# A gated mix of linear and softmax attention: output products and values stored from ScalarE's queue, head rows loaded in one transfer, 52 units of row maxima in the front instead of 56, and a new written order

## Chip, cores and metric

The kernel runs on 1 core of one Trainium2 chip. The metric is the device time of one execution in microseconds (us). Before the change it is 1009.66 us, the median of 3 runs (1009.21 to 1011.46).

## The reference

One sequence of S = 2048 tokens, D = 448 channels, H = 16 heads of 28. The output mixes two attentions of the same x by a gate for each token, all in fp32:

```
qkv = x @ wqkv                                   # for A and for B, each its own weights
A:  phi(u) = [softmax(u w_phi), softmax(-u w_phi)]          # 56 features for each head
    o = phi(q) (phi(k)^T v) / (phi(q) sum(phi(k)) + 1e-6);  a = o @ woA
B:  p = softmax(q k^T * 28^-0.5);  o = p v;                 b = o @ woB
g = sigmoid(sum(x * gate_w));  out = g * a + (1 - g) * b
```

## The kernel before

**Two parts.** The *front* (to about 333 us) computes everything of A, the projections of B, the gate, and a first share of B's row maxima. The *main loop* (s = 0 to 271, one *slot* each) computes B's attention: 4 groups of 4 heads x 4 blocks of 512 queries x 16 tiles of 128 keys are 256 slots. The products of the front are taken in split fp32r: each factor is written as a high and a low part, and high x high, high x low and low x high are summed (`x3`, L128, `tok_major`, L136).

**One slot of the main loop.** TensorE makes four score tiles `st` of 128 keys x 512 queries (`score_group`, L1010, matmul at L1048), ScalarE takes the exponential `p` (L1051), and TensorE adds the values, `pv` (`values`, L1136, matmuls at L1143). Key tiles are read from *stacks* `kst`: one stack holds four key tiles (512 keys) of one group; five stacks go round, and two query stacks `qst`. `stack` (L814) zero-fills one on POOL (L816), `load_k` (L835) and `load_q` (L825) load it from the scratch tensor `qk_d` in DRAM (L821, four transfers each), and the first one is copied from `qk0` (L838). Slots 0 to 3 use the first key stack, slots 4 to 7 the second (`kst1`), 8 to 11 the third, 12 to 15 the fourth. The values lie in `vb0` (key tiles 0 to 7) and `vb1` (8 to 15), loaded by `load_early` (L804, transfer at L808, 2048 KB each) from the scratch tensor `v_d`, into which `value_b` (L787) stored them tile by tile (`ve`, copied by ScalarE at L800, stored at L802).

**Row maxima.** The softmax of B subtracts the row maximum of q k^T, so the maxima of a block of queries are needed ahead of its scores. They are computed from q k^T a second time, in two forms that do the same work:

- in the front as *units* (`mx_unit`, L279): four matmuls at L305 into `pmb` and `pmd`, a relu by ScalarE (L312) of 128 x 1024, two fused add-and-max instructions of DVE (L314). NF = 56 units are in the front.
- in the main loop as *visits* (`mx_visit`, L329): four matmuls `pm` (L346), a relu by ScalarE (L350), two reductions and a fused one by DVE (L354, L357). The rest of the maxima are 200 visits: one in each slot below TWO = 167, beyond it one in each second slot.

The trick of both: max(a, b) = b + relu(a - b), with a - b from *differences of keys*. For a visit these are `kc` tiles: `mx_load` (L204) loads 28 rows of each of four heads (`mx_rows`, L191, transfers at L194), and POOL subtracts `kd` from one head's rows (L214, first to be used in visit s = 1, 2, 3 for `kc0_0`, `kc0_1`, `kc0_2`). Query rows are loaded likewise by `mx_query` (L221, `qc`).

**What sets the order.** The front's order is a list of strings, written by hand (from L940; each letter is a step, its number the tile): "o2.1" computes a tile of A's output (`out_a`, L628: the passes `poa`, then ScalarE multiplies by the gate into `ga`, L634, which is stored in `ga_d` at L635), "v15" a tile of values, "m", "c", "n", "r" parts of A's normalization (among them the products `oU` by `rsa`, L448, and the low parts `lo`, L592), "t" transposes (`turn`, L553), "z" loads the first stacks, "y" loads `vb0`, "l" opens the tiles for the last units. From "w" on, units are put between matmuls by a table `at` (L925): a unit goes in when as many passes (of 214) of outputs and values have been issued as its next number says. Engines other than SP run their instructions in this order. SP's order is made by the scheduler, and all transfers of this kernel, those of `ga`, `ve` and `vb` too, are issued by SP.

The order of the steps that open the main loop is also written out: four key stacks and a query stack are made (five fills), `load_k(0, 1)` and `load_early(1, 8)` follow, then the last two units and the scores of slot 0.

Of the kernel before, what the change touches and what calls it, by code (L numbers as in the profile page):

```python
# [29 lines left out]
NF = 56  # L30
# [10 lines left out]
def gated_mix_kernel(ctx, tc, xT, wqkB, wvB, wvA, wkAT, wqAT, phi, woA, woB,  # L41
# [34 lines left out]
    qk_d = dr.tile([2 * D, 2, S], F32, tag="qkd", name="qkd")  # L76
# [114 lines left out]
    def mx_rows(r, rows, src, heads, c):  # L191

        for i, j in zip(rows, heads):
            nc.sync.dma_start(f32(r[32 * i:32 * i + DH]), src[DH * j:DH * j + DH, 0, c:c + 512])  # L194
        return r
# [25 lines left out]
    def mx_query(gq):  # L221
        g, qb = divmod(gq, NQ)
        mxs[("qc", gq)] = mx_rows(mx_tile("qc", f"qc{gq}", 3), range(4), q_d[g], range(4), qb * 512)

    def pair_load(g, c):
# [5 lines left out]
        mx_rows(r, (0, 1), k_d[g], heads, b * 1024)  # L231
        mx_rows(r, (2, 3), k_d[g], heads, b * 1024 + 512)
        mx_rows(t, (2, 3), k_d[g], heads, b * 1024)
# [9 lines left out]
    def pair_query(gq, hp):  # L243
        g, qb = divmod(gq, NQ)
        mxs[("qp", gq, hp)] = mx_rows(mx_tile("qc", f"qp{gq}_{hp}", 3), range(4), q_d[g],
                                      (2 * hp, 2 * hp + 1) * 2, qb * 512)
# [381 lines left out]
    def out_a(n, a):  # L628
# [6 lines left out]
        nc.sync.dma_start(ga_d[n][a], ga)  # L635
# [56 lines left out]
    def first_units():  # L692
# [3 lines left out]
        for b in range(4):  # L696
            nc.sync.dma_start(raw[b][:, 0, :], wqkB[:, b, :512])
            nc.sync.dma_start(raw[b][:, 1, :], xT[:, b, :512])
# [4 lines left out]
        for _ in range(8):  # L703
# [30 lines left out]
    for n in range(4, NP):  # L734
# [9 lines left out]
        if n == 14:  # L744
            part_loads("wvA", wvA, 450, "wvA")
            nc.sync.dma_start(sel_s, sel)
            nc.vector.memset(gate1, -1.0)
# [39 lines left out]
    def value_b(t, mid=None):  # L787
# [13 lines left out]
        if t in EARLY:  # L801
            nc.sync.dma_start(v_d[:, k], v)  # L802

    def load_early(i, n):  # L804

        k = [t // 8 for t in EARLY].index(i)
        nc.gpsimd.memset(vb[i][:, 0, 0:1, 28:29], 1.0)
        nc.sync.dma_start(vb[i][:, :n].rearrange("p t h d -> p t (h d)"), v_d[:, k:k + n])  # L808
# [118 lines left out]
    do = {"p": query, "f": feature2, "t": turn, "v": value, "e": take_exps, "n": numer,  # L927
# [11 lines left out]
    for w in (  # L939
# [38 lines left out]
    TWO = 167  # L978
# [75 lines left out]
    kst += [stack(f"kst{i}", True) for i in range(1, 5)]  # L1054
    qst.append(stack("qst1", False))
# [4 lines left out]
    load_early(1, 8)  # L1060
# [313 lines left out]
```

## Time and profile before

| | |
|---|---|
| median of 3 runs | 1009.66 us (1009.21 to 1011.46) |
| the profiled execution | 1010.6 us, its span 1008.8 us, granted clock 0.998 |
| front, to the first scores `st` | 333.28 us of the span |
| main loop and end | 675.5 us of the span |
| busy: TensorE / ScalarE / VectorE / POOL | 990.9 / 794.6 / 674.2 / 233.4 us |

A row of a timeline gives the start, the length, the engine, line, operation, output and inputs of neighbouring instructions of one kind; the bracket is the idle time of the engine ahead of them and what ended it. A row of a table of stretches gives the window, its length, the busy time of PE, PEld (weight loads, beside PE), DVE, ACT and POOL with the number of instructions, the granted clock, the busy share of the DMA engines and GB/s. SPq is the time in which SP's queue issues transfers.

### The profile page before, as it was taken

The page shows a single profiled execution, that of the slowest core. Times are in us where ns is not written, and L with a number is a line of the kernel's source. Part 1 is how long each engine was busy: PE and PEld are TensorE (multiplying, and loading weights), DVE is VectorE, ACT ScalarE, POOL GpSimd, SP SyncE. Part 2 cuts the span into 40 slices and gives each one's busy share as a digit, 9 for nine tenths or more (in the row PEclk, how much of TensorE's full clock was granted, in tenths as well). Part 3 has the DMA queues.
Part 4 walks back from the last instruction along what each step waited for, and adds up shares of the span by engine and source line. Part 5 has one row for each costly group of instructions (what it writes and reads, how often), then busy time and mean ns, then how long its engine had stood idle before and what let it go on. Part 6 is the DMA issues. An engine that isn't in the chain of part 4 may idle for free.

```text
span 1008.8 us, 18258 instructions
## 1 busy us (share of the span) xinstructions
PE 990.9 (98%) x6604; PEld 549.4 (54%) x6604; DVE 674.2 (67%) x1351; ACT 794.6 (79%) x1491; POOL 233.4 (23%) x229
## 2 busy tenths in 40 slices
PE   9999999999998989999999999999999999999998
PEld 8877777898766433333333333333334444455656
DVE  6567767687857568888888788888886444544202
ACT  5456555544466889999999999999999999979672
POOL 1265445686811410210120101102011011101010
PEclk9999999999999999999999999999999999999999
DMA  8975220513358762332614323343233364315131
GB/s 301 317 248 176 97 88 31 191 62 101 107 153 241 211 144 49 79 77 60 129 59 109 78 51 90 85 110 90 62 86 76 82 127 107 89 37 148 62 104 55
DMA packets 73076, 115.18 MB, mean 114 GB/s; under 512 B 19641, under 2 KB 31593, under 8 KB 72713
## 3 DMA queue, kind: packets, MB, share of 16 engines
q1 hardware_dynamic: 72986, 114.02, 40.3%
q8 instruction: 52, 0.85, 0.4%
q14 instruction: 38, 0.31, 0.1%
HBM read 77.88 MB, written 35.68 MB: 113 GB/s over the span
## 4 chain that ended last, share of the span: by engine, by line
PE 89%; DVE 4%; DMA 3%; POOL 2%; issue 1%; ACT 1%; SPq 0%; DVEq 0%; POOLq 0%; ACTq 0%
PE st L1048 27%; PE pv L1143 24%; PE pm L346 8%; PE pqk L125 6%; PE pk L144 4%; PE pva L144 4%; PE pq L125 3%; PE pob L125 3%; PE pvb L144 2%; PE pmb L305 2%; PE poa L125 2%; PE pqk L722 1%; DMA kst<-qkd 1%; DMA vb<-vd 1%; PE pn L565 1%
## 5 line engine op out<-in xcount | busy, mean ns | idle before, releaser
L1051 ACT ACTIVATE p<-st 128x512 f32<-128x512 f32 x1020 | 527.7, 641 | 27.0 <-PE st L1048 26.8
L357 DVE TENSOR_REDUCE part<-pm 128x1 f32<-128x512 f32 x450 | 287.5, 685 | 157.4 <-PE pm L346 157.4
L1143 PE MATMUL pv<-p,vb 128*32 128x512 f32 x2048 | 264.5, 604 | 0.0
L350 ACT ACTIVATE rl<-pm 128x512 f32<-128x512 f32 x200 | 124.4, 622 | 18.8 <-PE pm L346 17.8
L346 PEld LDWEIGHTS pm<-kc,qc 28*128 28x128 f32 x800 | 38.8, 182 | 171.4 <-issue 100.6
L448 POOL TENSOR_TENSOR oUb<-oUb,rsb 128x512 f32<-128x512 f32 x15 | 19.3, 1289 | 457.1 <-DMA rsb<-rdb 138.6
L1048 PE MATMUL st<-qk,kst 128*128 128x512 f32 x384 | 116.9, 426 | 0.9 <-DVE part L357 0.9
L1048 PE MATMUL st<-qst,kst 128*128 128x512 f32 x384 | 114.9, 423 | 0.0
L346 PE MATMUL pm<-kc,qc 28*128 28x512 f32 x800 | 102.1, 496 | 2.8 <-POOL kc L214 2.8
L354 DVE CUSTOM_DVE_ANT_0 rl<-pm,rl 128x512 f32<-128x512 f32 x150 | 102.2, 681 | 0.0
L1143 PEld LDWEIGHTS pv<-p,vb 128*32 128x32 f32 x2048 | 47.4, 108 | 95.7 <-issue 88.9
L1048 PEld LDWEIGHTS st<-qk,kst 128*128 128x128 f32 x384 | 64.2, 188 | 39.4 <-ACT p L1051 16.8
L1048 PEld LDWEIGHTS st<-qst,kst 128*128 128x128 f32 x384 | 64.3, 187 | 38.1 <-ACT p L1051 16.6
L314 DVE CUSTOM_DVE_ANT_0 rl<-pmb,rl 128x512 f32<-128x512 f32 x72 | 46.0, 677 | 23.6 <-ACT rl L312 23.6
L125 PE MATMUL pqk<-XH,wB 128*128 128x512 f32 x192 | 59.6, 397 | 0.0
L312 ACT ACTIVATE rl<-pmd 128x1024 f32<-128x1024 f32 x36 | 37.0, 1027 | 25.5 <-PE pmd L305 16.5
L658 ACT CAST ev<-pqk 128x512 fp32r<-128x512 f32 x28 | 16.1, 587 | 36.2 <-PE pqk L125 30.0
L125 PEld LDWEIGHTS pqk<-XH,wB 128*128 128x128 f32 x192 | 35.4, 188 | 8.7 <-issue 1.7
L1158 DVE SCALAR_TENSOR_TENSOR acc<-pob,gate,acc 128x448 f32<-128x448 f32 x12 | 8.2, 684 | 47.1 <-PE pob L125 47.1
L1048 PE MATMUL st<-qk 128*128 128x512 f32 x124 | 37.7, 423 | 2.0 <-ACT p L1007 1.5
L125 PE MATMUL poa<-woA_s,hi 128*128 128x448 f32 x128 | 38.7, 377 | 0.3 <-ACT pcq L470 0.3
L144 PE MATMUL pk<-wkA_s,XH 128*128 128x448 f32 x128 | 38.9, 380 | 0.0
(167 smaller groups left out, 1373.6 us busy)
## 6 DMA issues: line engine op xcount, KB each, us to landing
qkd<-ev SPq DMA_DIRECT2D x28, 512.0 KB
qk<-qkd SPq DMA_DIRECT2D x48, 224.0 KB
kst<-qkd SPq DMA_DIRECT2D x48, 224.0 KB
qst<-qkd SPq DMA_DIRECT2D x32, 224.0 KB
od<-oTb SPq DMA_DIRECT2D x48, 112.0 KB
vd<-ve SPq DMA_DIRECT2D x16, 256.0 KB
rsa<-rda SPq DMA_DIRECT2D x32, 128.0 KB
vb<-vd SPq DMA_DIRECT2D x2, 2048.0 KB
```

Of the source, the lines that this page charges most:

```text
L125: nc.tensor.matmul(dst, l, r, start=i == 0, stop=i == len(todo) - 1, skip_group_check=mid is not None)
L144: nc.tensor.matmul(dst[:, :n], l, r, start=i == 0, stop=i == len(todo) - 1, skip_group_check=True)
L305: nc.tensor.matmul((pb if j < 2 else pd)[:, j % 2, :], qc[js, qt * P:(qt + 1) * P], kc[js, :], start=True, stop=True, tile_position=(32 * ...
L312: nc.scalar.activation(rl, pd, AF.Relu)
L314: nc.vector.tensor_tensor_reduce(rl[:, i, :], pb[:, i, :], rl[:, i, :], 1.0, LOWEST, ALU.add, ALU.max, part[:, col + i:col + i + 1])
L346: nc.tensor.matmul(pm[j], mxs[("qc", gq)][js, qt * P:(qt + 1) * P], mxs[("kc", g, kb)][js, :], start=True, stop=True, tile_position=(32 * ...
L350: nc.scalar.activation(rl, pm[kb], AF.Relu if kb < 3 else AF.Copy)
L354: nc.vector.tensor_tensor_reduce(r, pm[j], r, 1.0, LOWEST, ALU.add, ALU.max, part[:, col + j:col + j + 1])
L357: nc.vector.tensor_reduce(part[:, col + j:col + j + 1], pm[j], AX.X, ALU.max)
L1048: nc.tensor.matmul(st, kst_of[(gq // NQ, kt // 4)][:, j, (kt % 4) * P:(kt % 4 + 1) * P], qst_of[gq][:, j, :], start=True, stop=True)
L1051: nc.scalar.activation(p, st, AF.Exp, scale=SCALE)
L1143: nc.tensor.matmul(pv[32 * j:32 * j + 32, :], vb[kt // 8][:, kt % 8, 4 * g + j, :], pt[j], start=kt == 0, stop=kt == NT - 1, tile_position ...
```

## The change

Six things change.

1. NF goes from 56 to 52, TWO from 167 to 175: four units less in the front, four visits more in the main loop, in slots 167, 169, 171 and 173. The table `at` has 16 numbers instead of 20.
2. `mx_rows` loads the rows of n heads in one transfer of 32 n rows (28 of each head and 4 of the next), where their column offset is equal: `kd` 1 transfer instead of 3, `qc` 1 instead of 4, `kc` 2 to 4 instead of 4. `qk_d` has four more rows for that, filled from x.
3. The stores of `ga`, the stores of `ve` (now two tiles in one: 8 transfers of 512 KB instead of 16), the loads of `vb0` and `vb1` and that of the first block of x are issued by ScalarE: 27 transfers.
4. The front's order: a transpose "t11", "t12" and "m1" come sooner, "c1" and "c3" together behind "o1.0", "l" ahead of "o0.2", "j6" later, "y" directly behind "v15", other orders of the last outputs.
5. At the turn into the main loop only two fills (`kst1`, `kst2`) come ahead; `kst3`, `kst4` and `qst1` are made behind the visits of slots 1, 2 and 3. `vb1` is loaded in slot 2.
6. Six warm-up matmuls at the start instead of eight.

```
-NF = 56
+NF = 52
...
-    def mx_rows(r, rows, src, heads, c):
-        for i, j in zip(rows, heads):
-            nc.sync.dma_start(f32(r[32 * i:32 * i + DH]), src[DH * j:DH * j + DH, 0, c:c + 512])
+    def mx_rows(r, i, n, src, h, c, dc=0):
+        a = src[DH * h:DH * h + DH, 0, c:c + 512]
+        if n == 1:
+            nc.sync.dma_start(f32(r[32 * i:32 * i + DH]), a)
+            return r
+        row = a.ap[0][0]
+        nc.sync.dma_start(f32(r[32 * i:32 * (i + n)]), bass.AP(
+            a.tensor, a.offset, [[DH * row + dc, n], [row, 32], [1, 512]]))
         return r
...
         if c == 0:
             mxs["kd"] = mx_tile("kd", f"kd{g}", 1)
-            for h in range(3):
-                mx_rows(mxs["kd"], (h,), k_d[g], (h,), h * 512)
-        for h in range(4):
-            mx_rows(r, (h,), k_d[g], (h,), 512 * (c + (c == h and c < 3) - (c == h + 1 and c > 0)))
+            mx_rows(mxs["kd"], 0, 3, k_d[g], 0, 0, 512)
+        cs = [512 * (c + (c == h and c < 3) - (c == h + 1 and c > 0)) for h in range(4)]
+        h = 0
+        while h < 4:
+            n = 1
+            while h + n < 4 and cs[h + n] == cs[h]:
+                n += 1
+            mx_rows(r, h, n, k_d[g], h, cs[h])
+            h += n
...
-        nc.sync.dma_start(ga_d[n][a], ga)
+        nc.scalar.dma_start(ga_d[n][a], ga)
...
-            nc.sync.dma_start(raw[b][:, 1, :], xT[:, b, :512])
+            (nc.sync if b else nc.scalar).dma_start(raw[b][:, 1, :], xT[:, b, :512])
...
-        for _ in range(8):
+        for _ in range(6):
             nc.tensor.matmul(pqs[3][:, :P], ident, ident, start=True, stop=True)
...
-        if t in EARLY:
-            nc.sync.dma_start(v_d[:, k], v)
+        if t in EARLY and k % 2:
+            nc.scalar.dma_start(v_d[:, k - 1:k + 1], wB["ve"].rearrange("p t h d -> p t (h d)"))
...
-        nc.sync.dma_start(vb[i][:, :n].rearrange("p t h d -> p t (h d)"), v_d[:, k:k + n])
+        nc.scalar.dma_start(vb[i][:, :n].rearrange("p t h d -> p t (h d)"), v_d[:, k:k + n])
...
-        pace.update(n=0, at=[77, 92, 101, 104, 110, 115, 121, 127, 133, 139, 148, 155, 164, 169, 176, 181, 188, 195, 202, 209])
+        pace.update(n=0, at=[65, 79, 90, 102, 108, 116, 124, 133, 140, 147, 157, 164, 170, 190, 203, 210])
...
-    kst += [stack(f"kst{i}", True) for i in range(1, 5)]
-    qst.append(stack("qst1", False))
+    kst.append(stack("kst1", True))
+    nc.gpsimd.memset(vb[1][:, 0, 0:1, 28:29], 1.0)
+    kst.append(stack("kst2", True))
...
-    load_early(1, 8)
...
+            if s == 2:
+                load_early(1, 8)
...
+        if s in (1, 2):
+            kst.append(stack(f"kst{s + 2}", True))
+        if s == 3:
+            qst.append(stack("qst1", False))
```

**At the turn.** POOL's order before, from the one-column fill of `vb0` on, with the `kc` differences of the visits and the fills of the stacks:

```order
L807 MEMSET vb0_3014 128x1
L214 TENSOR_TENSOR kc0_0_3551<-kc0_0_3551,kd0_3552 28x512
L214 TENSOR_TENSOR kc0_1_3594<-kc0_1_3594,kd0_3552 28x512
L816 MEMSET kst1_3700 128x2048
L816 MEMSET kst2_3702 128x2048
L816 MEMSET kst3_3704 128x2048
L816 MEMSET kst4_3706 128x2048
L816 MEMSET qst1_3708 128x2048
L807 MEMSET vb1_3696 128x1
L214 TENSOR_TENSOR kc0_2_3636<-kc0_2_3636,kd0_3552 28x512
L214 TENSOR_TENSOR kc1_0_3887<-kc1_0_3887,kd1_3888 28x512
```

POOL's order of the changed kernel at the same place (its lines are L224 for a difference and L831 for a fill):

```order
L224 TENSOR_TENSOR kc0_0_3531<-kc0_0_3531,kd0_3532 28x512
L831 MEMSET kst1_3645 128x2048
L1071 MEMSET vb1_3641 128x1
L831 MEMSET kst2_3648 128x2048
L224 TENSOR_TENSOR kc0_1_3573<-kc0_1_3573,kd0_3532 28x512
L831 MEMSET kst3_3714 128x2048
L224 TENSOR_TENSOR kc0_2_3603<-kc0_2_3603,kd0_3532 28x512
L831 MEMSET kst4_3757 128x2048
L831 MEMSET qst1_3792 128x2048
L224 TENSOR_TENSOR kc1_0_3961<-kc1_0_3961,kd1_3962 28x512
```

The differences of `kc0_1` and `kc0_2` now stand between the fills; `kc0_1` has two fills ahead of it instead of none, `kc0_2` three instead of five.

SP's queue before, from the load of the second key stack on (`kd1`, `kc1_0` and `kc1_1` belong to the second group's visits):

```order
L838 DMA kst1_3700<-qk0_3379 1x16x128
L821 DMA kst1_3700<-qkd_68 28x4x512 x4
L808 DMA vb1_3696<-vd_74 128x4096
L838 DMA kst2_3702<-qk0_3379 1x16x128
L821 DMA kst2_3702<-qkd_68 28x4x512 x4
L838 DMA kst3_3704<-qk0_3379 1x16x128
L821 DMA kst3_3704<-qkd_68 28x4x512 x4
L194 DMA kd1_3888<-qkd_68 28x512 x3
L194 DMA kc1_0_3887<-qkd_68 28x512 x2
L194 DMA kc1_1_3925<-qkd_68 28x512 x4
```

SP's queue of the changed kernel from the same load on:

```order
L853 DMA kst1_3645<-qk0_3370 1x16x128
L836 DMA kst1_3645<-qkd_68 28x4x512 x4
L853 DMA kst2_3648<-qk0_3370 1x16x128
L836 DMA kst2_3648<-qkd_68 28x4x512 x4
L198 DMA qc4_3742<-qkd_68 128x1x512
L853 DMA kst3_3714<-qk0_3370 1x16x128
L836 DMA kst3_3714<-qkd_68 28x4x512 x4
L198 DMA kd1_3962<-qkd_68 96x1x512
L195 DMA kc1_0_3961<-qkd_68 28x512
L198 DMA kc1_0_3961<-qkd_68 96x1x512
```

`vb1` no longer stands between the first two stacks; ScalarE issues it. The rows of several heads (`128x1x512`, `96x1x512`) are one transfer each.

**In the front, the low parts.** VectorE's order before, around the low parts `lo0` and `lo2` of A's attention output (`oU`), with two transposes of query features (`fT1`):

```order
L592 TENSOR_TENSOR lo0_2852<-oU0_0_2573,hi0_0_2851 128x512
L553 STREAM_TRANSPOSE fT1_2693<-feat3_482 128x1024
L448 TENSOR_TENSOR oU0_0_2573<-oU0_0_2573,rsa2_2754 128x1024
L472 TENSOR_REDUCE extq14_2892<-pcq14_2890 128x16
L473 TENSOR_REDUCE extq14_2892<-pcq14_2890 128x16
L553 STREAM_TRANSPOSE fT1_2693<-feat0_479 128x1024
L592 TENSOR_TENSOR lo2_2898<-oU0_0_2573,hi0_0_2851 128x512
```

VectorE's order of the changed kernel around the same two (its lines are L605, L566 and L461):

```order
L566 STREAM_TRANSPOSE fT1_2687<-feat3_481 128x1024
L485 TENSOR_REDUCE extq13_2826<-pcq13_2824 128x16
L486 TENSOR_REDUCE extq13_2826<-pcq13_2824 128x16
L605 TENSOR_TENSOR lo0_2846<-oU0_0_2568,hi0_0_2845 128x512
L461 TENSOR_TENSOR oU0_0_2568<-oU0_0_2568,rsa2_2748 128x1024
L566 STREAM_TRANSPOSE fT1_2687<-feat0_478 128x1024
L485 TENSOR_REDUCE extq14_2885<-pcq14_2883 128x16
L486 TENSOR_REDUCE extq14_2885<-pcq14_2883 128x16
L605 TENSOR_TENSOR lo2_2890<-oU0_0_2568,hi0_0_2845 128x512
```

The transpose of `feat3` moved ahead of `lo0`, so that one transpose instead of two stands between the low parts, and ahead of the reductions.

**At the front's end.** ScalarE's order of the changed kernel at its last value tile (before, its queue held no transfer):

```order
L814 COPY ve14_3315<-pvb15_3389 128x16x28
L816 DMA vd_74<-ve14_3315 128x1024
L823 DMA vb0_3006<-vd_74 128x4096
L325 ACTIVATE rl_s_3081<-pmd43_3419 128x1024
L325 ACTIVATE rl_s_3081<-pmd44_3435 128x1024
L647 ACTIVATE ga3_1_3445<-poa3_1_3414,z_s_84 128x448
L648 DMA gad3_72<-ga3_1_3445 128x448
```

The store of two value tiles, the load of `vb0` and the stores of A's output now stand among the relus of the units and the products `ga`.

More of the change, by code (lines that the diff above doesn't have):

```diff
@@ L74, in scratch @@
         return [dr.tile(shape, F32, tag=f"{nm}{i}", name=f"{nm}{i}") for i in range(NG)]
-    qk_d = dr.tile([2 * D, 2, S], F32, tag="qkd", name="qkd")
+    qk_d = dr.tile([2 * D + 4, 2, S], F32, tag="qkd", name="qkd")
     q_d = [qk_d[g * GW:(g + 1) * GW] for g in range(NG)]
@@ L222, in mx_query @@
         g, qb = divmod(gq, NQ)
-        mxs[("qc", gq)] = mx_rows(mx_tile("qc", f"qc{gq}", 3), range(4), q_d[g], range(4), qb * 512)
+        mxs[("qc", gq)] = mx_rows(mx_tile("qc", f"qc{gq}", 3), 0, 4, q_d[g], 0, qb * 512)
     def pair_load(g, c):
@@ L230, in pair_load @@
         t = mx_tile("kd", f"kt{g}_{c}", 1)
-        mx_rows(r, (0, 1), k_d[g], heads, b * 1024)
-        mx_rows(r, (2, 3), k_d[g], heads, b * 1024 + 512)
-        mx_rows(t, (2, 3), k_d[g], heads, b * 1024)
+        for i in range(4):
+            mx_rows(r, i, 1, k_d[g], heads[i % 2], b * 1024 + i // 2 * 512)
+        for i in (2, 3):
+            mx_rows(t, i, 1, k_d[g], heads[i % 2], b * 1024)
         mxs[("kp", g, c)] = r
@@ L244, in pair_query @@
         g, qb = divmod(gq, NQ)
-        mxs[("qp", gq, hp)] = mx_rows(mx_tile("qc", f"qp{gq}_{hp}", 3), range(4), q_d[g],
-                                      (2 * hp, 2 * hp + 1) * 2, qb * 512)
+        r = mx_tile("qc", f"qp{gq}_{hp}", 3)
+        for i in range(4):
+            mx_rows(r, i, 1, q_d[g], 2 * hp + i % 2, qb * 512)
+        mxs[("qp", gq, hp)] = r
     def mx_fin():
@@ L746, in gated_mix_kernel @@
             nc.sync.dma_start(sel_s, sel)
+            nc.sync.dma_start(qk_d[2 * D:, 0, :], xT[:4, 0, :])
             nc.vector.memset(gate1, -1.0)
@@ L924, in units_open @@
     def units_open():
-        pace.update(n=0, at=[77, 92, 101, 104, 110, 115, 121, 127, 133, 139, 148, 155, 164, 169, 176, 181, 188, 195, 202, 209])
-    do = {"p": query, "f": feature2, "t": turn, "v": value, "e": take_exps, "n": numer,
+        pace.update(n=0, at=[65, 79, 90, 102, 108, 116, 124, 133, 140, 147, 157, 164, 170, 190, 203, 210])
+    vals = list(range(NT))
+    do = {"p": query, "f": feature2, "t": turn, "v": lambda n: value(vals.pop(0)), "e": take_exps, "n": numer,
           "r": norm2, "m": norm3, "c": part_of, "o": lambda n, a: out_a(n, a), "u": mx_unit,
@@ L977, in gated_mix_kernel @@
     NS = NG * NQ * NT
-    TWO = 167
+    TWO = 175
     slots = {"n": 0}
```

3 lines of the change are left out of this document (2 added, 1 removed), and 14 rows, old and new, of the table woA_s.

## The prediction

> **What bounds the kernel now.** First the head of the page, for the span and for the engine that fills it.
>
> ```profile
> span 1008.8 us, 18258 instructions
> PE 990.9 (98%) x6604; PEld 549.4 (54%) x6604; DVE 674.2 (67%) x1351; ACT 794.6 (79%) x1491; POOL 233.4 (23%) x229
> ```
>
> TensorE is busy in 98%, so this change pays only where TensorE stands still, or where it runs fewer or cheaper matmuls. The second view is the table of stretches: length, then busy time (and count) of PE, weight loads, DVE, ACT and POOL, the granted clock, DMA share and GB/s. The stretches are the main loop far from its ends, the front's last part (cut at 306 us), the turn into the main loop, and two microseconds of that turn.
>
> ```profile
> 600.00:700.00 100.00, 100.00 (x623) 38.47 (x623) 81.03 (x163) 96.80 (x195) 13.33 (x12) 1.00 0.36 89
> 261.00:306.00 45.00, 39.96 (x421) 29.35 (x420) 32.65 (x56) 25.78 (x38) 18.09 (x16) 1.00 0.51 149
> 306.00:333.30 27.30, 25.20 (x135) 17.52 (x135) 18.49 (x56) 17.52 (x22) 4.33 (x4) 1.00 0.75 228
> 333.30:372.00 38.70, 33.47 (x189) 13.41 (x191) 23.39 (x49) 31.51 (x61) 13.88 (x10) 0.96 0.73 193
> 364.00:366.00 2.00, 2.00 (x13) 0.71 (x11) 2.00 (x4) 1.97 (x5) 1.32 (x2) 0.78 0.46 137
> ```
>
> The main loop has no hole to fill. The holes are in the front (5.04 + 2.10 = 7.14 us of idle PE) and in the turn (5.23 us, and a clock under 1.00). Third, the timeline of TensorE over the turn: start, length, instructions, and in brackets the idle time ahead and its releaser.
>
> ```profile
> 333.28 1.08 PE L999 MATMUL st<-qk 128*128 128x512 f32 x4
> 336.78 1.07 PE L1143 MATMUL pv<-p,vb 128*32 128x512 f32 x8
> 343.79 0.83 PE L346 MATMUL pm<-kc,qc 28*128 28x512 f32 x4 [0.76 <-POOL kc L214]
> 363.01 0.70 PE L346 MATMUL pm<-kc,qc 28*128 28x512 f32 x4 [2.02 <-POOL kc L214]
> 371.73 1.06 PE L1143 MATMUL pv<-p,vb 128*32 128x512 f32 x8
> ```
>
> The front ends, and the first scores start, at 333.28. Two visits wait for POOL's `kc` (key differences), 0.76 and 2.02 us. Fourth, the chain of waits through the turn, and POOL's timeline beside it.
>
> ```profile
> 334.19 1.94 DMA gad<-ga
> 342.41 7.93 DMA vb<-vd
> 350.71 9.27 DMA kst<-qkd
> 359.99 1.71 DMA kc<-qkd
> 361.71 1.26 POOL kc L214
> ```
>
> ```profile
> 333.55 7.04 POOL L816 MEMSET kst<- 128x2048 f32 x4 [4.64 <-PE poa L125]
> 340.55 1.80 POOL L816 MEMSET qst<- 128x2048 f32 x1
> 361.71 2.60 POOL L214 TENSOR_TENSOR kc<-kc,kd 28x512 fp32r<-28x512 f32 x2 [17.98 <-DMA kc<-qkd]
> ```
>
> One story: five fills hold POOL for 8.8 us while a key difference waits behind them, and SP's queue brings `vb` and `kst` (7.93 + 9.27 us) ahead of the next `kc`, whose difference TensorE then awaits at 363.01.
>
> **The turn.** In the main loop one slot (scores of one key tile, values, one visit) has this length.
>
> ```profile
> 500.94 1.06 PE L1143 MATMUL pv<-p,vb 128*32 128x512 f32 x8
> 501.94 0.51 PE L346 MATMUL pm<-kc,qc 28*128 28x512 f32 x4
> 506.15 1.07 PE L1143 MATMUL pv<-p,vb 128*32 128x512 f32 x8
> ```
>
> Two slots take 506.15 - 500.94 = 5.21, so 2.605 each. From 336.78 to 371.73 stand eleven slots, 34.95 against 11 x 2.605 = 28.66: 6.3 us lost, the slow clock after the 2.02 us gap included. In the changed order `kc0_2`'s difference follows three fills rather than five, and three of the four stacks are asked for in slots 1 to 3. Three fills of 1.76 (7.04 / 4) and three differences of 1.3 (2.60 / 2), begun 0.3 behind the front's end, make it ready 9.5 us behind that end; its visit, which without its wait would have begun at 343.03, wants it at 9.75. `vb1` leaves SP's queue, so `kst2` and the group-1 keys come up to 8 us sooner. I keep 0.5 us of the stall (small margins): **-5.8**. Bounds: all of it goes (-6.3); or the 2.02 gap with its slow clock and most else stays (-2.5).
>
> **The four visits.** Units that leave the front come back as visits in the main loop, at slots 167, 169, 171 and 173. The chain of waits beyond slot 167 shows two slots that share one visit.
>
> ```profile
> 776.04 2.16 PE st L1048 x8
> 780.49 2.15 PE st L1048 x8
> ```
>
> 4.45 against 5.21 with two: a visit costs 0.76, four **+3.0**. TensorE's own share is the 0.51 of the row at 501.94, so +2.0 at the least.
>
> **The front.** Its price list, on TensorE's timeline: a unit (four row matmuls, two pairs at once) among projection passes.
>
> ```profile
> 321.36 0.36 PE L125 MATMUL poa<-woA_s,lo 128*128 128x448 f32 x1
> 321.56 0.36 PE L125 MATMUL poa<-woA_s,hi 128*128 128x448 f32 x1
> 321.85 0.50 PE L305 MATMUL pmb<-kp,qp 28*128 28x512 f32 x2
> 322.28 0.47 PE L125 MATMUL poa<-woA_s,hi 128*128 128x448 f32 x1
> 322.59 0.37 PE L125 MATMUL poa<-woA_s,lo 128*128 128x448 f32 x1
> ```
>
> Passes without a unit start 0.20 apart (321.36 to 321.56); from 321.56 to 322.59 are two passes and a unit, so a unit is 1.03 - 0.40 = 0.63. Four fewer: **-2.5**, and nothing covers it, since TensorE is the engine that ends the front. The other front terms are holes.
>
> ```profile
> 265.08 0.47 PE L125 MATMUL poa<-woA_s,lo 128*128 128x448 f32 x1 [1.29 <-DVE lo L592]
> 307.97 0.50 PE L305 MATMUL pmb<-kp,qp 28*128 28x512 f32 x2 [0.98 <-DVE part L314]
> 318.03 0.50 PE L305 MATMUL pmb<-kp,qp 28*128 28x512 f32 x2 [1.12 <-DVE part L314]
> ```
>
> The first is cut by the new place of a transpose: DVE ran it just ahead of the `lo` that TensorE awaited.
>
> ```profile
> 263.00 1.23 DVE L553 STREAM_TRANSPOSE fT<-feat 128x1024 f32<-128x1024 f32 x1
> 264.16 0.87 DVE L592 TENSOR_TENSOR lo<-oU,hi 128x512 fp32r<-128x512 f32 x1
> ```
>
> With both late transposes a step up the order, `lo2` comes 1.16 us (264.16 - 263.00) sooner: **-1.2**. The other two are DVE still at work on the last unit's maxima. The pace list now spreads 16 units instead of 20 over the same 214 passes, so DVE has a quarter more time for each, and of the 2.10 idle here I take off **-1.3**. One unit fewer on DVE ahead of `lo6`, two of these each:
>
> ```profile
> L314 DVE CUSTOM_DVE_ANT_0 rl<-pmb,rl 128x512 f32<-128x512 f32 x72 | 46.0, 677 | 23.6 <-ACT rl L312 23.6
> ```
>
> is 1.35 us, of which I take **-1.0**, since the reciprocals that `lo6` needs also come by SP's queue. Sum of the front: -2.5 - 1.2 - 1.3 - 1.0 = **-6.0**, between -2.5 (units alone; the holes move) and -8 (nearly all 7.14 of idle go, and some units' price).
>
> Against this stand some 19 transfers that ACT now issues. No DMA on ACT is in this trace; the nearest rows are SP's.
>
> ```profile
> 334.19 0.34 SPq L635 DMA_DIRECT2D gad<-ga  x1
> 274.38 2.53 SPq L635 DMA_DIRECT2D gad<-ga  x2
> ```
>
> 0.34 to 1.27 each. I take 0.4, as in the row where nothing is ahead: 10 in the last 27.3 us are 4 us, in 9.8 us of ACT's idle time there (27.30 - 17.52), and four units' relus fall out. So I cost them at nothing; at 1.27 the cover is gone. `vd`'s halved count and the merged loads relieve SP, which waits for no one here.
>
> **The start.** `x`'s first block leaves from ACT instead of from behind SP's first load:
>
> ```profile
> 0.74 0.40 SPq L697 DMA_DIRECT2D first_raw<-in_wqkB_dram  x1
> 1.19 0.42 SPq L698 DMA_DIRECT2D first_raw<-in_xT_dram  x1
> ```
>
> 0.45 sooner, if ACT is free; two warm-up matmuls fewer must not be in the way either. I take **-0.3**, between 0 and -0.45. The pad rows of `qk_d` are one small transfer, far from any wait: nothing.
>
> **Sum.** -0.3 - 6.0 - 5.8 + 3.0 = -9.1. The profiled execution took 1010.6 (span 1008.8 and 1.8 around it), so 1001.5; it lies 0.94 over the median of 1009.66, so **1000.6**. Ends: -0.45 - 8 - 6.3 + 2.0 = -12.75, and 0 - 2.5 - 2.5 + 3.0 = -2.0: 996.9 to 1007.7.
>
> **Rivals.** (A) *ScalarE's issues eat the front's gain*: each costs near 1.27, relus come late, holes stay: front 0, total -3.1, 1006.6. For it: DVE's maxima wait for ACT's relu (the 23.6 of the row of L314), so what delays ACT delays them. Against: 17.52 of 27.30 busy.
>
> (B) *Slower: every transfer of ACT waits for an older one to land.* In the emitted order each carries a wait on the counter of an earlier transfer, which its row shares. If it has to sit out a landing (1.94, the `gad` row of the chain), then ten in the last 27.3 us are 19.4 on top of 17.52 of work: 36.9, so +9.6 in place of -6.0, total +6.5, 1016.2. It decides from 0.98 us a transfer, (27.30 - 17.52) / 10. Against: the older one was mostly issued several microseconds before.
>
> (C) *The stall moves*: `vb1`, `kst2` and `kst3` are still the same bytes. They took 17.6 us (342.41 to 359.98); asked for from some 5 us behind the front's end, they are whole at about 22.5. The first values stand 3.5 behind that end, so `vb1` is wanted eight slots on, at 24.3, and `kst2`, for scores a slot and a half sooner, at 20.5. If half the stall stays (-3.0 in the turn), or late group-1 keys take its place: -6.3, 1003.4 to 1005. For it: the DMA share of 0.73 in the turn. Against: `kst2` has a head start on `vb1`. On this the Trainium skill speaks against the change: "DMA: Bandwidth & Descriptors", section "Rules for kernel authors", says that spreading transfers over SP, ACT and GpSimd brings no bandwidth, as all use the same 16 DMA engines, and saves issue time alone. The 17.6 us are bandwidth if that holds, and the sum is 2.0 worse (22.5 against 20.5), 1002.6; by issue order alone it is 1000.6.
>
> (D) *Merged loads run thin.* A transfer of two to four heads may land later than its pieces did (1.71, the `kc` row of the chain). If a piece of 262 KB (four heads, 128 rows of 2 KB) moves at a quarter of the turn's 193 GB/s, it takes 5.4, and the early visits wait up to 3.7: 1004.3. The skill has the rule, in the same page's "Why a DMA increments its semaphore by 16 and not by 1": a transfer uses the largest number up to 16 that divides both sides' slowest dimension, so four heads by 32 rows would run on 4 engines; no row here has such a transfer.
>
> (E) *The change doesn't take*: other releasers stand close behind in the front and the turn, only +3.0 and the units' -2.5 remain: 1010.2.
>
> **Chances.** Forecast 0.53, A 0.12, B 0.09, C 0.14, D 0.07, E 0.05. A measurement of this kernel can tell about 0.2%, 2 us, from no change. A, C and D are all faster by more; E is the same; with the ends of the terms I give faster 0.85, same 0.06, slower 0.09. The range, 996.5 to 1007.7, leaves out B, E and what lies past the ends.
>
> **What would show it.** On TensorE's timeline the first scores should start near 327 (right: 326 to 329; A or E: 333; B: over 340), and eleven slots behind the first values take under 30 us (C: over 31.5), with no 2 us wait on `kc` and a clock of 1.00. `pm` waits on `kc` of a merged load would show D. ACT's queue rows show what one issue costs: near 0.4 right, over 0.98 B. Each of slots 167, 169, 171 and 173 should be 0.76 longer. The prediction fails if ACT's issues cost over 1 us, or if the stacks come late.

## The result and the profile after

The changed kernel takes **1025.39 us** (median of 4 runs, 1022.42 to 1025.77) against 1010.44 beside it: a ratio of **1.0142** (95% interval 1.0119 to 1.0166). The forecast was 1000.6, the range 996.5 to 1007.7, and slower had 0.09. The profiled execution took 1025.6 us.

The head of the page of the changed kernel: the span is 14.8 us longer, TensorE is busy 5.7 us longer (slow-clock matmuls among it; their clock is shown below), and the rest of the difference is idle time.

```profile
span 1023.6 us, 18145 instructions
PE 996.6 (97%) x6600; PEld 550.8 (54%) x6600; DVE 678.0 (66%) x1351; ACT 793.2 (77%) x1491; POOL 233.6 (23%) x229
```

TensorE's timeline of the changed kernel, over the turn (the first scores; the third, fourth, twelfth and eighteenth `pv` behind them; the waits):

```profile
332.85 1.20 PE L1015 MATMUL st<-qk 128*128 128x512 f32 x4
341.35 1.06 PE L1159 MATMUL pv<-p,vb 128*32 128x512 f32 x8
343.14 0.81 PE L359 MATMUL pm<-kc,qc 28*128 28x512 f32 x4 [0.72 <-POOL kc L224]
354.96 2.04 PE L1064 MATMUL st<-qk,kst 128*128 128x512 f32 x4 [10.59 <-DMA kst<-qkd]
356.93 1.94 PE L1159 MATMUL pv<-p,vb 128*32 128x512 f32 x8
378.62 1.07 PE L1159 MATMUL pv<-p,vb 128*32 128x512 f32 x8
390.56 2.04 PE L1064 MATMUL st<-qst,qk 128*128 128x512 f32 x4 [2.52 <-DMA woB_raw<-in_woB_dram]
399.53 1.07 PE L1159 MATMUL pv<-p,vb 128*32 128x512 f32 x8
```

The third, fourth and eighteenth `pv` of the kernel before, whose twelfth (371.73) the prediction shows:

```profile
341.96 1.06 PE L1143 MATMUL pv<-p,vb 128*32 128x512 f32 x8
346.19 1.07 PE L1143 MATMUL pv<-p,vb 128*32 128x512 f32 x8
387.26 1.06 PE L1143 MATMUL pv<-p,vb 128*32 128x512 f32 x8
```

Set against each other, these rows hold the result. The front ends 0.43 us sooner (333.28 to 332.85). The third `pv` is 0.61 sooner, the fourth 10.74 **later**: slot 4's scores wait 10.59 us for `kst1`, and behind the wait the clock is halved for 4 us. The twelfth is 6.89 later: 3.85 us come back, in spite of the slow stretch, since the old stall of the turn (2.02 us at 363 and the slow clock behind it) is indeed gone. Then slot 16 waits 2.52 us, another slow stretch follows, and the eighteenth `pv` is 12.27 later. From there to the end 624.07 us pass (1023.6 - 399.53) against 621.54 (1008.8 - 387.26): the four visits, 2.53.

The slow clock is seen in the table of stretches of the changed kernel (third figure from the end: 0.62 and 0.70 in the front, 0.50 behind each of the two waits):

```profile
300.00:305.00 5.00, 3.82 (x11) 2.26 (x12) 5.00 (x10) 3.08 (x4) 1.70 (x1) 0.62 0.50 144
305.00:310.00 5.00, 5.00 (x22) 3.40 (x21) 4.91 (x9) 3.33 (x5) 1.32 (x2) 0.70 0.29 96
355.00:357.00 2.00, 2.00 (x8) 1.16 (x12) 0.00 (x0) 1.18 (x3) 0.00 (x0) 0.50 0.71 171
392.00:394.00 2.00, 2.00 (x10) 0.20 (x8) 0.00 (x0) 1.49 (x4) 0.00 (x0) 0.50 0.33 106
```

**Who holds kst1.** In the kernel before, SP issues the four pieces of `kst1` in one go and `vb1` 3 us behind them:

```profile
337.38 1.88 SPq L821 DMA_DIRECT2D kst<-qkd  x4
342.41 0.35 SPq L808 DMA_DIRECT2D vb<-vd  x1
```

The chain of waits of the changed kernel at slot 4, then the rows of ScalarE's and of SP's queue beside it:

```profile
336.02 5.95 DMA kc<-qkd
341.99 12.84 DMA kst<-qkd
```

```profile
337.75 0.34 ACTq L823 DMA_DIRECT2D vb<-vd  x1
```

```profile
336.02 0.52 SPq L198 DMA_DIRECT2D kc<-qkd  x1
338.20 4.09 SPq L836 DMA_DIRECT2D kst<-qkd  x4
```

Two suspects stand in these lines. `vb1`'s 2 MB leave ScalarE's queue at 337.75, ahead of all four pieces of `kst1` (338.20 to 342.29); the written order puts that load into slot 2, and ScalarE issues it when it comes to that place, while SP still has `kc` rows to issue. And the merged `kc` rows issued at 336.02 (two heads, 128 KB) take 5.95 us to land; `kst1`'s last piece shares their completion counter in the emitted program and leaves only then (341.99 in the chain). Theory 1 blames the overtaking, theory 2 the merged transfers.

### The profile page after: what moved, and what is told of

It reads as the page before. It is cut to its first block, busy times and chain, and to the rows that moved or that the text cites. A ratio compares the mean times of both kernels' runs of the same rounds, so it can differ in the third digit from the quotient of the medians.

```text
span 1023.6 us, 18145 instructions
## 1 busy us (share of the span) xinstructions
PE 996.6 (97%) x6600; PEld 550.8 (54%) x6600; DVE 678.0 (66%) x1351; ACT 793.2 (77%) x1491; POOL 233.6 (23%) x229
## 4 chain that ended last, share of the span: by engine, by line
PE 93%; DMA 5%; DVE 1%; ACT 1%; issue 0%; SPq 0%; POOL 0%; ACTq 0%; DVEq 0%
PE st L1064 27%; PE pv L1159 24%; PE pm L359 8%; PE pqk L125 6%; PE pk L144 4%; PE pva L144 4%; PE pq L125 4%; PE pvb L144 3%; PE poa L125 3%; PE pob L125 3%; PE pmb L318 2%; DMA kst<-qkd 1%; PE pn L578 1%; PE pqk L735 1%; DMA rsa<-rda 1%; DMA qst<-qkd 1%
## 5 line engine op out<-in xcount | busy, mean ns | idle before, releaser
L370 DVE TENSOR_REDUCE part<-pm 128x1 f32<-128x512 f32 x459 | 293.3, 685 | 159.7 <-PE pm L359 159.7
L363 ACT ACTIVATE rl<-pm 128x512 f32<-128x512 f32 x204 | 127.1, 623 | 19.6 <-PE pm L359 18.4
L461 POOL TENSOR_TENSOR oUb<-oUb,rsb 128x512 f32<-128x512 f32 x15 | 19.3, 1287 | 510.5 <-DMA rsb<-rdb 212.5
L359 PE MATMUL pm<-kc,qc 28*128 28x512 f32 x816 | 104.4, 497 | 0.7 <-POOL kc L224 0.7
L125 PE MATMUL poa<-woA_s,hi 128*128 128x448 f32 x128 | 40.9, 394 | 3.5 <-ACT hi L604 1.8
L1064 PE MATMUL st<-qst,qk 128*128 128x512 f32 x128 | 40.1, 434 | 2.5 <-DMA woB_raw<-in_woB_dram 2.5
```

The costliest lines, as they stand in the source:

```text
L125: nc.tensor.matmul(dst, l, r, start=i == 0, stop=i == len(todo) - 1, skip_group_check=mid is not None)
L359: nc.tensor.matmul(pm[j], mxs[("qc", gq)][js, qt * P:(qt + 1) * P], mxs[("kc", g, kb)][js, :], start=True, stop=True, tile_position=(32 * ...
L363: nc.scalar.activation(rl, pm[kb], AF.Relu if kb < 3 else AF.Copy)
L370: nc.vector.tensor_reduce(part[:, col + j:col + j + 1], pm[j], AX.X, ALU.max)
L1064: nc.tensor.matmul(st, kst_of[(gq // NQ, kt // 4)][:, j, (kt % 4) * P:(kt % 4 + 1) * P], qst_of[gq][:, j, :], start=True, stop=True)
```

## The experiments

A run's ratio is always to the kernel before, run beside it. A timeline is that of one execution, so a wait of a few tenths differs from one profile to the next.

**1. vb1 back on SP.**

```
-        nc.scalar.dma_start(vb[i][:, :n]...
+        (nc.sync if i else nc.scalar).dma_start(vb[i][:, :n]...
```

> The changed kernel, with vb1's load issued by SP again, behind the loads of kst1 and kst2. Theory 1 (vb1's 2 MB leave ScalarE's queue at 337.75, just ahead of kst1's pieces at 338.20 to 342.29, and share the DMA engines with them): the 10.6 us wait of TensorE on kst1 at slot 4 falls to under 2 us, the clock stays at 1.00 there, and the time falls by about 11 us to 1014. Theory 2 (kst1 is late because its last piece waits for the merged rows of kc0_3, which took 5.95 us to land): the wait stays at 7 us or more, and the time falls by under 4 us. Both leave the second wait, of slot 16 on qst1 (2.5 us and some 3 us of slow clock).

1018.83 us, ratio 1.0084 (1.0055 to 1.0114). TensorE's timeline of this run, the waits at slots 4 and 16:

```profile
345.18 2.05 PE L1064 MATMUL st<-qk,kst 128*128 128x512 f32 x4 [3.96 <-DMA qc<-qkd]
383.69 2.04 PE L1064 MATMUL st<-qst,qk 128*128 128x512 f32 x4 [5.50 <-DMA woB_raw<-in_woB_dram]
```

The wait falls from 10.59 to 3.96: most of it is vb1's overtaking, but 4 us are left, more than theory 1 alone allows, and the time is 5 us above theory 1's 1014. The second wait has grown.

**2. vb1 on ScalarE, two slots later.**

```
-            if s == 2:
+            if s == 4:
                 load_early(1, 8)
```

> The changed kernel, with vb1's load still on ScalarE, two slots later (slot 4 instead of 2). Theory 1: kst1's 0.9 MB have landed or nearly so by then, and the wait at slot 4 falls to under 2 us; vb1 is wanted about 14 us behind its issue and shares them with kst2, so up to 2 us may come back at slot 8; about 1014 to 1016. Theory 2: the wait at slot 4 stays at 7 us or more.

1018.98 us, ratio 1.0105 (1.0065 to 1.0145). The wait is about that of run 1, so it is the moment and not the queue that counts: the load left 0.9 us behind `kst1`'s last piece, whose issue ended at 339.59.

```profile
345.20 2.04 PE L1064 MATMUL st<-qk,kst 128*128 128x512 f32 x4 [4.18 <-DMA kst<-qkd]
340.44 0.33 ACTq L823 DMA_DIRECT2D vb<-vd  x1
```

Theory 1 had said under 2 us here too.

**3. Each head's rows apart again.**

```
-        nc.sync.dma_start(f32(r[32 * i:32 * (i + n)]), bass.AP(... [[DH * row + dc, n], [row, 32], [1, 512]]))
+        for m in range(n):
+            b = src[DH * (h + m):DH * (h + m) + DH, 0, c + dc * m:c + dc * m + 512]
+            nc.sync.dma_start(f32(r[32 * (i + m):32 * (i + m) + DH]), b)
```

> The changed kernel, with each head's 28 rows loaded by a transfer of their own again. Theory 2: the last piece of kst1 is issued at about 340 instead of 342, and the wait at slot 4 falls by 4 us or more, the time to 1019 or less. Theory 1: the wait stays between 8 and 12 us, and the time within 3 us of the changed kernel's 1025.

1016.0 us, ratio 1.0062 (1.0039 to 1.0084). Its timeline has one wait left, and none at slot 16:

```profile
351.39 2.04 PE L1064 MATMUL st<-qk,kst 128*128 128x512 f32 x4 [7.63 <-DMA kst<-qkd]
```

Each expectation misses in part: the wait loses 3 us (theory 2 said 4 or more), and the time falls by 8, by the ratios (theory 1 said under 3), since the second wait goes too. The two theories hold side by side.

**4. A's output products stored from SP.**

```
-        nc.scalar.dma_start(ga_d[n][a], ga)
+        nc.sync.dma_start(ga_d[n][a], ga)
```

> The changed kernel, with A's output products stored from SP again. Theory 3 (in the front SP's loads of the reciprocals wait for the landing of ga stores, since counters are shared by both queues, and a 4.5 us hole with a clock of 0.6 to 0.7 follows at 297 to 310): the hole shrinks to under 2 us, the first scores start at 327 to 329 instead of 332.85, and the time falls by 3 to 6 us. If the hole comes from the new order alone: the first scores stay within 1 us of 332.85. The wait on kst1 may change as well, since SP's order changes at the turn.

1035.99 us, ratio 1.0254 (1.0223 to 1.0286), the slowest of all. Theory 3 gets no support: the first scores come at 342.62, since ScalarE's next `ga` waits for the landing of a store that SP's queue now issues late (ScalarE's and TensorE's timelines of this run):

```profile
329.86 0.63 ACT L647 ACTIVATE ga<-poa,z_s 128x448 f32<-128x448 f32 x1 [9.05 <-DMA gad<-ga]
330.55 1.12 PE L125 MATMUL poa<-woA_s,hi 128*128 128x448 f32 x2 [7.19 <-ACT ga L647]
```

The run isn't a clean test of the hole at 297 us, because SP's whole order moved. It shows what these stores cost on SP beside the change's other transfers. The new written order alone doesn't need them off SP: run 10 has it with every transfer on SP and no such wait.

**5. Both suspects undone** (the edits of runs 1 and 3).

> The changed kernel with both suspects undone: vb1's load on SP behind kst1 and kst2, and each head's rows by a transfer of their own. Theory 1+2 (vb1's overtaking and the thin merged transfers each hold kst1, and the thin ones alone make slot 16 wait): the wait at slot 4, 10.6 us in the changed kernel, 4.0 with vb1 on SP, 7.6 with the rows apart, falls to 0 to 2 us; slot 16 doesn't wait; the time is 1004 to 1008, below the kernel before. If something else delays kst1 (the later fill, the counter waits of SP): the wait stays at 3 to 4 us and the time at 1009 to 1012.

1010.89 us, ratio 1.0011 (0.9997 to 1.0025). All but 1 of the 14 us are gone, so these two are the cause of the loss. But 2.55 us of the wait stay, the time is that of the expectation's other case, where something else delays kst1 as well (run 9), and nothing is gained on the kernel before:

```profile
331.18 1.20 PE L1015 MATMUL st<-qk 128*128 128x512 f32 x4
345.12 1.17 PE L1064 MATMUL st<-qk,kst 128*128 128x512 f32 x4 [2.55 <-DMA kst<-qkd]
```

As a two-by-two table, in ratios: neither 1.0011, vb1 alone 1.0062, merged rows alone 1.0084, both 1.0142. vb1 costs 5.2 us, the merged rows 7.4, both together 13.2 (differences of the ratios times 1010): they nearly add up.

**6. The same with the start as before** (x's first block on SP, eight warm-up matmuls).

```
-            (nc.sync if b else nc.scalar).dma_start(raw[b][:, 1, :], xT[:, b, :512])
+            nc.sync.dma_start(raw[b][:, 1, :], xT[:, b, :512])
-        for _ in range(6):
+        for _ in range(8):
```

> As the kernel with both suspects undone, and the start as before too: x's first block from SP, eight warm-up matmuls. If the new start costs (weights land 1.3 us later because x's block shares the DMA engines with them, and TensorE idles 1.1 to 1.6 us ahead of its first product, in some runs with slow matmuls behind it): the first product starts at 4.8 instead of 5.4 to 5.8, the forty-first of the first projection at 11.2 instead of 11.0 to 13.2, and the time is 0 to 2 us lower. If the start is neutral: the same time within 0.5 us.

1010.1 us, ratio 1.0000 (0.9989 to 1.0011). The first product starts at 4.79 again; the time is 0.8 lower, within the intervals of both. The new start isn't seen to gain, and that it loses isn't shown in the time either.

**7. The kernel before with merged rows alone** (change 2, nothing else).

> The kernel before with the merged head loads alone. Theory 2 (each merged transfer runs on as many DMA engines as it has heads): the loads of kc1 take about 5 us each, the difference that TensorE awaited at 363 comes 3 us later, and the time rises by 3 to 8 us. If merging only saves SP's issue time: the time falls by 0 to 2 us.

1018.78 us, ratio 1.0084 (1.0059 to 1.0110): 8.5 us from the merging alone, a little above the range that theory 2 gave. Its timeline shows where; the third row is the wait that stood at 363, 9.5 us later as counted from the first scores (expected: 3), since two longer waits have come ahead of it.

```profile
349.89 1.11 PE L359 MATMUL pm<-kc,qc 28*128 28x512 f32 x4 [2.88 <-POOL kc L224]
355.30 2.05 PE L1062 MATMUL st<-qk,kst 128*128 128x512 f32 x4 [3.57 <-DMA kst<-qkd]
374.17 0.51 PE L359 MATMUL pm<-kc,qc 28*128 28x512 f32 x4 [2.07 <-POOL kc L224]
```

**8. The kernel before with 52 units and 175 alone.** The expectation names the new table, but this run's edit leaves the old table `at` of 20 numbers in place; with four units less its last four numbers find none, and the last unit starts at 324.04 instead of 331.72 (331.34 in the changed kernel).

```
-NF = 56
+NF = 52
-    TWO = 167
+    TWO = 175
```

> The kernel before with 52 units and their new table, and 175 for 167, alone. By the prediction's prices: the front 2.5 us shorter or more (the first scores at 330 to 331 instead of 333.3), four visits 3.0 us more, in all -1 to +1 us, if the turn stays as it is.

1010.19 us, ratio 1.0000 (0.9984 to 1.0015): within the range expected. The first scores come at 331.39, 1.9 us sooner (the four units at 0.63 are 2.5). The turn, which is the old one, is 1.9 us shorter too, with no visit waiting for `kc` any more, and the four visits cost 2.9 (table in the next section). That the units' sooner end brings the `kc` rows in time is likely and not tested alone. What the new table does is not tested by this run.

**9. kc0_2 and kc0_3 behind kst1** (on run 6: `mx_load` of c = 2 and 3 moves from the last units to slot 0, ahead of `load_k(0, 2)`).

```
-        if gq == GM and qt == QM - 1:
+        if gq == GM and qt == QM - 1 and c < 2:
             mx_load(g, c)
...
+            if s == 0:
+                for c in (2, 3):
+                    mx_load(0, c)
+                diffs[-1] = (NF - 1, diffs[-1][1])
```

> As the run with both suspects undone and the old start, and the loads of kc0_2 and kc0_3 asked for behind kst1's instead of ahead of them in SP's queue. If the rest of the wait at slot 4 (2.5 to 2.8 us and some slow clock) is SP's issue time (eight loads of kc rows, 0.4 us each, stand ahead of kst1, which leaves at 337 with 331 as the front's end): kst1 leaves 3 us sooner, the wait falls to under 0.5 us, and the time is 3 to 4 us lower, 1006 to 1007, faster than both kernels. If it is the transfers' bandwidth: the wait stays over 2 us and the time at 1010.

1009.36 us, ratio 0.9984 (0.9971 to 0.9997), above the 1006 to 1007 expected. `kst1`'s four pieces leave from 334.92 on instead of 338.38 (run 6), and the last one lands in 6.1 us as before (6.2): its wait is gone, and a visit waits instead. Its bracket names a transfer, but POOL's row below shows the cause: `kc0_2`'s difference has waited 2.70 us for its loads.

```profile
344.64 1.11 PE L359 MATMUL pm<-kc,qc 28*128 28x512 f32 x4 [2.92 <-DMA kst<-qk]
```

```profile
343.33 1.25 POOL L224 TENSOR_TENSOR kc<-kc,kd 28x512 fp32r<-28x512 f32 x1 [2.70 <-DMA kc<-qkd]
```

So SP's issue time, about 0.4 us a transfer, does set when `kst1` comes, and the two waits nearly trade places.

**10. The kernel before with run 8's edit and the new written order, all transfers on SP.** Here too the old table stays, other than the expectation says.

```
+    vals = list(range(NT))
-            "j6", "k12", "f-1", "u", "p0", ...
+            "k12", "f-1", "u", "p0", ...
```

> The kernel before with 52 units, their table, 175 for 167 and the new written order of the front, with all transfers on SP; the turn is as before, so only the front is read from it. The run with the units alone ended the front at 331.4. If the new order gains what the prediction gave it (1.2 for lo2, 1.0 for lo6): the first scores start at 329 to 330. If its holes only move, as in the changed kernel: 331 to 333.

One run, 1013.16 us. The first scores come at 333.79, 2.4 us later than with the units alone. Its timeline shows two longer waits, both for low parts, which the order was to bring sooner (`lo2`, then one that POOL makes):

```profile
264.92 0.47 PE L125 MATMUL poa<-woA_s,lo 128*128 128x448 f32 x1 [1.90 <-DVE lo L592]
319.38 0.47 PE L125 MATMUL poa<-woA_s,lo 128*128 128x448 f32 x1 [1.70 <-POOL lo L592]
```

In this one profile the new order loses against run 8, which differs from it in the order alone. With ScalarE's transfers, the new table and the new start the same order ends at 331.18 (run 5) and at 332.38 with the old start (run 6), so it is no gain over run 8 there either; what of this is the queue, the table or the start is not shown.

**11. kc0_3 alone behind kst1**, and **12. the same with an earlier unit table.**

```
-        if gq == GM and qt == QM - 1:
+        if gq == GM and qt == QM - 1 and c < 3:
...
+            if s == 0:
+                mx_load(0, 3)
```

```
-        at=[..., 164, 170, 190, 203, 210]
+        at=[..., 164, 170, 182, 194, 206]
```

> As the run with both suspects undone and the old start, with kc0_3's four loads alone asked for behind kst1's; kc0_2's stay ahead. If SP's issue time sets the turn (1.6 us for four loads): kst1 leaves 1.6 us sooner than in the run with eight loads ahead of it, where TensorE waited 2.84 us, and its wait falls to about 1 us without the 2.9 us wait for kc0_2 that came with eight loads behind it; the time is 1007 to 1009. If the two waits only trade places: 1009 to 1010.

> The same with the last three numbers of the unit table 182, 194, 206 for 190, 203, 210, so that the kc loads that units release are asked for up to 3 us sooner. If SP's issue time and the release of kc's buffers set the turn: kst1 leaves at once behind its fill, both waits go, 1006 to 1008. If VectorE gets too little time for the closer units: a hole of 1 us or more in the last 10 us of the front, and no gain.

Run 11: 1008.52 us, ratio 0.9981 (0.9969 to 0.9994). Run 12: 1007.98 us, ratio 0.9987 (0.9973 to 1.0001). Both lie a little below the kernel before; that the earlier table gains on run 11 isn't shown. The wait at slot 4 was 2.46 us in the profile of run 11 (expected: 1; the bracket names nothing that ended it) and under 1 us in that of run 12, where slot 16 waits instead:

```profile
344.70 1.52 PE L1064 MATMUL st<-qk,kst 128*128 128x512 f32 x4 [2.46 <-issue]
343.81 1.17 PE L1064 MATMUL st<-qk,kst 128*128 128x512 f32 x4 [0.84 <-DVE part L370]
377.43 2.05 PE L1064 MATMUL st<-qst,qk 128*128 128x512 f32 x4 [1.95 <-DMA qc<-qkd]
```

Runs 9 and 11 are below both kernels, below the one before by 0.16 and 0.19%, which is no more than the bound of what the prediction called measurable.

## Why the prediction was wrong

Three stages of the profiled executions, in us; the turn here is the stretch from the first scores to the eighteenth `pv`, the rest what follows to the end:

| | front | turn | rest |
|---|---|---|---|
| kernel before | 333.28 | 53.98 | 621.54 |
| changed kernel | 332.85 | 66.68 | 624.07 |
| merged rows alone of the two suspects (run 1) | 330.09 | 61.27 | 624.24 |
| vb1 alone of the two suspects (run 3) | 332.42 | 57.72 | 624.06 |
| neither (run 5) | 331.18 | 52.90 | 624.12 |
| before, merged rows alone (run 7) | 334.92 | 61.78 | 621.00 |
| before, 52 units and 175 alone (run 8) | 331.39 | 52.09 | 624.42 |

The prediction's low end is 996.9 by its own sum and 996.5 in its range; the measured time lies far above either.

- **The turn (-5.8, was +12.7).** This is the step that failed. Its sentence "`vb1` leaves SP's queue, so `kst2` and the group-1 keys come up to 8 us sooner" looked at what stood behind `vb1` in SP's queue, and not at what `vb1` itself would pass by leaving it: `kst1`, for which I set no time at all. The old stall did go, and 0.72 us of the first wait for `kc` stayed, nearly as before. Two waits that weren't there took its place: eleven slots behind the first values took 42.57 us (336.05 to 378.62) instead of under 30. The other half of the failed step is "the merged loads relieve SP, which waits for no one here": the sum put them at nothing, and they cost 7.4 to 8.5 us. And without both suspects (run 5) the turn is only 1.1 us shorter than before, not 5.8; part of the rest went into the 2.55 us that `kst1` still kept slot 4 waiting and a slow clock behind it (0.50 from 347 to 349). One reading was wrong as well: the prediction has three of the four key stacks asked for in slots 1 to 3, but only the fills of `kst3`, `kst4` and `qst1` moved there, and `kst1`, the first one wanted, is filled and asked for ahead of slot 0 as before.
- **Rival C** had the right mechanism (the same bytes at the same time) on the wrong stack. I let it decide between `kst2` and `vb1`, with "a head start" for `kst2`; `kst1` had the opposite, 0.45 us behind. Run 1 removes 6.6 us of its wait by the place of the load alone. The rule that C quotes from the Trainium skill ("DMA: Bandwidth & Descriptors", section "Rules for kernel authors"), that another queue brings no bandwidth, agrees with the trace: with 2 MB on ScalarE's queue ahead of them, TensorE waited 6.6 us longer for SP's 0.9 MB.
- **Rival D** was right and priced at half: 3.7 foreseen, 7.4 to 8.5 measured (runs 1 to 5, and 7). I had it act on the early visits; it acts on what comes behind, first `kst1`, whose last piece waits for a merged load to land, then `qst1` at slot 16 (both waits are shorter or gone in run 3). In the changed kernel a load of three heads (192 KB) was issued at 364.23 and its difference began at 369.75. The strip of the DMA engines' busy share in 40 slices of the 6 us from 364 to 370, and what was moved:

```profile
DMA  2222222612112221121221212122212112221111
DMA packets 233, 0.46 MB, mean 77 GB/s; under 512 B 15, under 2 KB 15, under 8 KB 232
q1 hardware_dynamic: 232, 0.44, 20.4%
```

  The 0.46 MB are more than twice this load, so it isn't alone in the stretch; `kd1`'s rows, three heads too and issued at 358.52, are the likeliest other part. 20.4% of 16 engines is 3.3 engines. That is near the number that the Trainium skill gives ("DMA: Bandwidth & Descriptors", section "Why a DMA increments its semaphore by 16 and not by 1": the largest number up to 16 that divides the slowest dimension of both sides, here 3 and 96). The clearest pair is a load of four heads' query rows `qc` in a quiet stretch of the main loop. The kernel before does it with four transfers, the first issued at 704.24; the changed kernel with one, issued at 553.12. Both strips begin 0.24 us ahead of the issue and hold 10 us in 40 slices (704 to 714, before; 552.88 to 562.88, changed):

```profile
DMA  1100015734440000000000000000000000003927
```

```profile
DMA  1411003311212222222100000002816899986200
```

  Four transfers keep mostly three to seven tenths of the engines busy and are done 3 us behind the first issue; one keeps one to three tenths busy and is done after 5 us.

- **The front (-6.0, was -0.43).** The units' -2.5 came as 1.9 (run 8). The order's terms failed: `lo2`'s 1.29 us fell to 0.39, and 2.2 us behind it a wait of 1.13 for ScalarE's copy of a value tile stood in its place; the holes on DVE's maxima went from 4.0 us in all to 0.3 (2.2 in run 2, where the clock stayed at 1.00, so a slow TensorE probably hides part of them here), and one hole at 299 to 302 us took over, behind the loads of the reciprocals `rsa` (changed kernel; waits, then the chain):

```profile
264.26 0.47 PE L125 MATMUL poa<-woA_s,lo 128*128 128x448 f32 x1 [0.39 <-DVE lo L605]
266.46 0.68 PE L125 MATMUL poa<-woA_s,hi 128*128 128x448 f32 x2 [1.13 <-ACT ve L814]
300.91 0.91 PE L125 MATMUL poa<-woA_s,hi 128*128 128x448 f32 x2 [1.76 <-ACT hi L604]
```

```profile
287.58 3.16 DMA gad<-ga
292.21 5.01 DMA rsa<-rda
297.24 3.71 DMA rsa<-rda
```

  In that chain SP's reciprocals wait, through a shared counter, for a `ga` store of ScalarE to land (3.16). That link is read from the trace and the emitted program and was not tested alone. It can be a small part only: in run 2, the same front, these loads leave SP at 291.83 instead of 292.21, and VectorE has them at 296.74 instead of 298.98. There no wait of TensorE from 294 to 310 is longer than 1.07 us, the clock is 1.00 from 300 to 310, and the first scores come at 329.89 instead of 332.85. So some 3 us hang on that hole and the slow clock behind it; why the loads land later in one execution than in another stays open.
- **ScalarE's issues (0.4 each, was 0.33).** Right for the issue itself, and with it the cause that A gave falls: 0.33 us is far from 1.27. B's landings are there but few: from 261 to 333 us ScalarE waited for the landing of a store four times, 6.2 us in all, where B had 1.94 us ahead of every transfer (the second row is one of the four). A's outcome for the front (no gain) came about all the same, by the holes above.

```profile
305.68 0.33 ACTq L648 DMA_DIRECT2D gad<-ga  x1
315.31 1.14 ACT L604 CAST hi<-oU 128x512 fp32r<-128x512 f32 x2 [1.41 <-DMA vd<-ve]
```

- **The start (-0.3, was +0.2).** x's block left 0.46 sooner, at the same moment as the first weights, and both were used later: the first casts of ScalarE (weights) and VectorE (x) begin at 5.16 and 4.97 instead of 3.52 and 4.19. That the two transfers share the engines is the likely cause and wasn't tested alone. TensorE stood idle where the warm-up matmuls used to reach, and the first eight products ended at 7.95 instead of 7.78 (4.79 + 2.99).

```profile
5.83 2.12 PE L735 MATMUL pqk<-XH,wB 128*128 128x512 f32 x8 [1.55 <-ACT wB L720]
```

  In runs 3 and 4 the same eight products took 3.75 us instead of 2.12. They vary without an idle stretch too: 2.99 in the kernel before, 2.09 in run 6. So that the idle stretch makes them slow isn't shown.
- **The four visits (+3.0, was +2.53).** Right; 2.5 to 2.9 in every run that has them and whose stages are in the table.
- **Rival E** (the change doesn't take, 1010.2, chance 0.05) is what is left without the two suspects: 1010.89 in run 5.

## What to carry over

When a load moves to another queue, set its new time of issue against every load that it now passes, not only against those that it no longer delays; a load on another queue leaves when that engine comes to it (here at slot 2), however much the first queue still has to issue. Before merging small loads into one, count the DMA engines that the merged pattern can use: fewer issues on the queue can mean a transfer several times thinner, and whatever follows it pays. And a stall that several transfers share moves on when one of them is cured (runs 9 and 12): price a turn by its last transfer, not by its first.

## What the runs showed of the hardware

- One transfer of four heads' rows (256 KB, outermost dimension 4) kept one to three tenths of the 16 DMA engines busy and was done about 5 us behind its issue at 553.12; four transfers of 28 rows each (224 KB in all) reached three to seven tenths and were done 3 us behind the first issue at 704.24.
- 2 MB issued on one queue 0.45 us ahead of 0.9 MB on another made TensorE wait 10.59 us for the latter; issued 0.9 us behind them, on the same queue as before, 4.18 (run 2).
- Waits of TensorE well below 3 us were followed by a slow clock. In the front, 1.76 us (changed kernel) was followed by a granted clock of 0.62 and 0.70 over the next 10 us, and 1.24 us (run 1) by 0.66 over 5; where no wait was longer than 1.07 us (run 2) the clock stayed at 1.00. Yet 2.02 us at 363 in the kernel before was followed by 0.50 (366 to 368), and 2.07 us at 374 in run 7 by 1.00. The wait of 10.59 us was followed by 4 us at half the clock.
- The first eight products took 2.1 us in some runs and 3.75 in others behind an idle TensorE of 1.1 to 1.6 us, and 2.99 and 2.09 behind none, with a granted clock of 1.00 in the table of stretches each time.
